# The second-last tile of a fused attention and MLP kernel, computed with tokens on the output partitions

## The chip, the cores and the metric

The kernel runs on one core of a Trainium2 chip. A core has five engines with an instruction stream each: TensorE (PE, matrix products), VectorE (DVE), ScalarE (ACT), GpSimd (POOL) and SyncE (SP, which here only starts transfers). ACT starts transfers too. Sixteen DMA engines move the data between the on-chip memory SBUF and the device memory. Matrix products are accumulated in PSUM, eight banks of 128 partitions by 512 float32.

The metric is the device time of one execution in microseconds. A profile of one execution shows what each engine did; its span runs from the first to the last recorded work, and the time of that execution is a little longer than the span.

## The reference

Polysketch attention over 4 batches, 4 heads, 1088 tokens and head size 32, and behind it a two-layer network with a leaky rectifier on the 4352 tokens of 128 features:

```python
def phi(x):
    a = np.einsum('rd,bhsd->bhsr', S1, x)
    b = np.einsum('rd,bhsd->bhsr', S2, x)
    return np.einsum('bhsi,bhsj->bhsij', a, b).reshape(*x.shape[:-1], r * r)
q_p, k_p = phi(q), phi(k)
kv = np.einsum('bhsf,bhsd->bhfd', k_p, v)
z = np.sum(k_p, axis=2)
num = np.einsum('bhsf,bhfd->bhsd', q_p, kv)
den = np.einsum('bhsf,bhf->bhs', q_p, z)[..., None] + 1e-06
x = (num / den).transpose(0, 2, 1, 3).reshape(B * S, H * D)
h = x @ w_in                                  # 128 -> 2048
g = np.maximum(h, 0.0) + alpha * np.minimum(h, 0.0)
out = g @ w_out                               # 2048 -> 128
```

## The kernel before

The kernel rewrites the rectifier as a linear part and a plain relu: `out = x @ W + relu(x @ w_in) @ ((1 - alpha) * w_out)` with `W = w_in @ (alpha * w_out)`. W is made on the chip (step Wmm and W).

**Steps of attention.** For each batch b the keys go through `k{b}T` (a transpose on DVE), `k{b}ab` (a product on PE, the two sketches), `k{b}abT`, two products `k{b}kp0` and `kp1` on POOL or DVE, the sums `z{b}` and `kv{b}` on PE, and `zm`, `zM`, `zW`, `kvc`, `fin`, `kvW`, which bring the sums into the form that the queries use. Queries go through `q{b}T`, `q{b}f` (PE), `fT`, `denm`, `den`, `rec`, `ph`, `phT` (DVE and POOL) and `q{b}num` (PE, line 838), and `q{b}x` copies the result to SBUF as the tile's input. Batch 0 is cut in parts (q0.a, q0.b, q0.1), since it starts while the inputs still arrive.

**Steps of the network.** `mlp` (from line 962) does one tile of tokens g, ten in all: tiles 0 to 5 and 7 have 512 tokens, 6, 8 and 9 have 256. d_ff is cut in 16 chunks. `h{g}.{c}` (line 982) is the first product of a chunk, with the weights stationary and up to 512 tokens streaming, into one PSUM bank; in tiles of 256 tokens two chunks share a bank. `r{g}.{c}` is the relu of that bank, on ACT (line 989) or DVE (line 991), to a bf16 buffer rh. `o{g}.{c}` (line 1004) is the second product, all chunks of which are added up in one bank, and `W{g}`, the linear part, is added to the same bank. The result of these tiles stands with the 128 output features on the partitions. `oT{g}` (line 1013, DVE) transposes it in blocks of 32 on its way to SBUF, and `st{g}` (`store_main`, line 1029) writes it with four transfers, one for each block of 32 features, so that one piece in device memory is 32 floats, 128 bytes. Tile 8's four transfers go two from SP and two from ACT.

Tile 9, the last, is done differently (`final`, line 1002): there the relu's output is stationary and the weights stream, 128 columns at a time, so that the result has tokens on the partitions. It takes twice as many matmuls of half the length, two PSUM banks, two plain copies (`oT9.0` on DVE, `oT9.1` on ACT, line 396 and 394) and two transfers with 512 bytes in one piece (`store_last`, line 1042), one from SP (`st9.0`) and one from ACT (`st9.1`).

**What sets the order.** A planner in the kernel (`plan`, line 188 on) orders all steps before any instruction is issued. Each step has a due time, worked back from its users, to which the table `SHIFT` adds a number for each step by name; a table `PIN` fixes the engine of some steps that two engines can do. The planner places steps by due time, by assumed durations, and by free buffers. Instructions then stand in that order on each engine, and each engine takes them strictly in order. SP's list holds all big loads and stores, ACT's the four small loads, the relus, copies and its stores. Loads of the weights from w_in1 on are released by the step zM0, those of batch 2 by kv1.0 and those of batch 3 by k2ab. The planner counts PE's instructions in blocks of 256 (`BLOCK`, `BEFORE`, line 58), because it reckons with the fetch of instructions; before the first tile it fills PE with warm-up matmuls (line 544).

The tile's own buffers: `po` is the bank for the second product (at most three at a time), `ph` a bank for a chunk (at most four), `oT__91` and `oT__92` in the profile are output buffers in SBUF, `ft__73` and `ph__75` are buffers of attention that tile 9 reuses.

Of the kernel before, what the change touches and what calls it, by code (L numbers as in the profile page):

```python
# [34 lines left out]
class Op:  # L35
# [274 lines left out]
def kernel(  # L310
# [12 lines left out]
    nc = tc.nc  # L323
# [41 lines left out]
    def ps(b):  # L365
        return PS[:, b.slot] if b.n == 1 else PS[:, b.slot:b.slot + b.n]

    def sb(b):
        return tiles[b.cls][b.slot]
# [592 lines left out]
    def mlp(g, n, xs, needs, bx, store, final=False, lat=5000):  # L962
# [32 lines left out]
        for i, (name, cs, z, dep, br, t) in enumerate(hs):  # L995
            def om(e, i=i, cs=cs, br=br, z=z):
                for q, c in enumerate(cs):
                    y, w = (xs(), W_bf) if c == NC else (sb(br)[:, q * np:q * np + np], w3[:, c, 0])
                    first, last = i + q == 0, i == len(hs) - 1 and c == cs[-1]
                    if final:  # L1000
                        for j in range(n // 128):
                            nc.tensor.matmul(ps(bos[j])[:, :128], y[:, 128 * j:128 * j + 128], w, start=first, stop=last)
# [118 lines left out]
```

## Time and profile before

| | |
|---|---|
| median of 3 runs | 105.85 us (105.42, 105.85, 107.14) |
| the profiled execution | 105.28 us |
| its span | 103.3 us |
| PE busy | 94.0 us, 91% |
| DVE, ACT, POOL busy | 83.9, 62.4, 43.1 us |
| granted clock of TensorE | 0.995 |
| moved by DMA | 11.83 MB, 26916 packets, of which 19988 under 512 bytes |

The page gives, in its parts, the busy time of each engine; the span in 40 slices of 2.6 us, with tenths of busy time for each engine; the DMA queues (q1 belongs to SP's transfers, q10 to ACT's, q8 and q14 carry instructions); the chain of work that ended last, by engine and line, where SPq and ACTq mean the issuing of a transfer; and the costliest groups of instructions. PE lists matmuls and PEld loads of stationary weights; both are TensorE instructions. In timelines a row is start in us, duration in us, engine, line, operation, output and input tiles, shapes and count; a bracket gives the idle time ahead and what ended it. The duration of several merged instructions is from the first start to the last end.

Matmuls of 512 columns follow each other every 0.217 us, and a pair of 256 takes the same. PE's last matmul starts at 98.69 us.

### The profile page before, as it was taken

The numbers are of one execution on the slowest core, as the hardware profiler recorded it, in microseconds if no ns is written. First come the engines' busy times: TensorE is split into PE (matmuls) and PEld (weight loads), VectorE is DVE, ScalarE is ACT, GpSimd is POOL, SyncE is SP. The second block draws the span as 40 slices with busy tenths as digits, with TensorE's granted clock in tenths as the row PEclk, the third lists the DMA queues.
The fourth block names the chain that finished last, engine by engine and source line by source line (L and its number), as shares of the span: only waits on it lengthen the run. The fifth ranks groups of instructions, "written<-read, shape, count | busy, mean of one in ns | idle before, by whom it ended". The sixth has DMA issues, their size and how long they took to land.

```text
span 103.3 us, 3390 instructions
## 1 busy us (share of the span) xinstructions
PE 94.0 (91%) x1374; PEld 54.7 (53%) x1384; DVE 83.9 (81%) x160; ACT 62.4 (60%) x134; POOL 43.1 (42%) x43
## 2 busy tenths in 40 slices
PE   7999898499799999999999999999999999999930
PEld 2348676276445745344364455554444765568920
DVE  6777789698978999799998959798896799849910
ACT  0604598997234896696296727746873757584610
POOL 3186885792896080195049239309900000000000
PEclk9999999999999999999999999999999999999997
DMA  2996689999002970199860001640000412410632
GB/s 33 341 260 161 221 259 342 367 196 167 14 6 74 381 191 8 19 341 271 122 111 0 0 0 27 114 74 0 0 0 9 75 24 41 83 30 5 109 51 53
DMA packets 26916, 11.83 MB, mean 115 GB/s; under 512 B 19988, under 2 KB 25364, under 8 KB 26900
## 3 DMA queue, kind: packets, MB, share of 16 engines
q1 hardware_dynamic: 25920, 11.44, 45.7%
q10 hardware_dynamic: 980, 0.16, 0.9%
q8 instruction: 11, 0.18, 0.7%
q14 instruction: 5, 0.04, 0.1%
HBM read 8.85 MB, written 2.23 MB: 107 GB/s over the span
## 4 chain that ended last, share of the span: by engine, by line
PE 76%; DMA 7%; DVE 6%; SPq 3%; issue 3%; ACTq 2%; ACT 0%; DVEq 0%
PE ps L982 27%; PE ps L1004 25%; DMA q<-in_q_dram 7%; PE ps L544 5%; PE ps L838 4%; PE ps L722 3%; PE ps L676 3%; PE ps L793 3%; SPq L417 3%; ACTq L1029 2%; PE ps L638 2%; DVE pt__77 L827 1%; DVE qT__71 L778 1%; PE ps L713 1%; PE ps L762 1%
## 5 line engine op out<-in xcount | busy, mean ns | idle before, releaser
L982 PEld LDWEIGHTS <-w_in_bf 128*128 128x128 bf16 x176 | 16.5, 98 | 14.1 <-issue 2.3
L1004 PEld LDWEIGHTS <-w 128*128 128x128 bf16 x160 | 15.4, 99 | 12.1 <-issue 1.6
L982 PE MATMUL ps<-xT__96,w_in_bf 128*128 128x512 bf16 (+1 forms) x78 | 19.8, 336 | 0.4 <-ACT xT__96 L394 0.2
L982 PE MATMUL ps<-xT__95,w_in_bf 128*128 128x512 bf16 (+1 forms) x79 | 18.8, 336 | 0.6 <-POOL w_in_bf L398 0.2
L989 ACT ACTIVATE rh__83<-ps 128x512 bf16<-128x512 f32 x17 | 10.3, 605 | 4.8 <-PE ps L982 3.4
L692 POOL TENSOR_TENSOR kp__68<-ab__66 128x1152 f32<-128x1152 f32 (+1 forms) x5 | 8.6, 1735 | 10.9 <-DVE ab__66 L679 8.9
L989 ACT ACTIVATE rh__84<-ps 128x512 bf16<-128x512 f32 x15 | 9.0, 598 | 3.8 <-PE ps L982 3.7
L989 ACT ACTIVATE rh__85<-ps 128x512 bf16<-128x512 f32 x15 | 9.0, 599 | 3.0 <-PE ps L1004 1.6
L1004 PE MATMUL ps<-rh__83,w 128*128 128x256 bf16 (+1 forms) x32 | 9.1, 326 | 0.2 <-issue 0.2
L824 POOL TENSOR_TENSOR ph__76<-ft__73 128x1280 f32<-128x1280 f32 x3 | 7.2, 2393 | 3.3 <-DVE ph__75 L824 3.3
L989 ACT ACTIVATE rh__86<-ps 128x512 bf16<-128x512 f32 x12 | 7.2, 601 | 1.6 <-PE ps L982 0.8
L1004 PE MATMUL ps<-rh__84,w 128*128 128x256 bf16 (+1 forms) x28 | 8.0, 325 | 0.2 <-issue 0.2
L544 PE MATMUL ps<-const-bfloat16-1.0 128*128 128x512 bf16 (+4 forms) x23 | 6.4, 380 | 0.9 <-PEq L1105 0.8
L991 DVE TENSOR_SCALAR rh__83<-ps 128x512 bf16<-128x512 f32 x9 | 6.1, 678 | 1.0 <-PE ps L982 0.8
L798 DVE STREAM_TRANSPOSE ft__73<-ps 128x576 f32<-128x576 f32 (+1 forms) x8 | 5.4, 703 | 1.8 <-PE ps L793 1.7
L989 ACT ACTIVATE rh__88<-ps 128x512 bf16<-128x512 f32 x11 | 6.6, 603 | 0.1
L692 POOL TENSOR_TENSOR kp__69<-ab__66 128x1152 f32<-128x1152 f32 x3 | 6.5, 2178 | 0.0
L838 PE MATMUL ps<-pt__77,kvW 32*32 32x256 f32 (+3 forms) x256 | 5.9, 372 | 0.6 <-DVE pt__77 L827 0.6
L1004 PE MATMUL ps<-rh__85,w 128*128 128x256 bf16 (+1 forms) x23 | 6.5, 323 | 0.0
L1004 PE MATMUL ps<-rh__86,w 128*128 128x512 bf16 (+1 forms) x21 | 6.5, 338 | 0.0
L991 DVE TENSOR_SCALAR rh__84<-ps 128x512 bf16<-128x512 f32 (+1 forms) x9 | 5.9, 653 | 0.4 <-PE ps L1004 0.2
L824 POOL TENSOR_TENSOR ph__75<-ft__73 128x1024 f32<-128x1024 f32 x2 | 3.9, 1950 | 5.4 <-DVE ft__73 L813 5.3
(175 smaller groups left out, 201.6 us busy)
## 6 DMA issues: line engine op xcount, KB each, us to landing
v<-in_v_dram SPq DMA_DIRECT2D x12, 144.0 KB, 5.8
k<-in_k_dram SPq DMA_DIRECT2D x3, 544.0 KB, 3.8
q<-in_q_dram SPq DMA_DIRECT2D x3, 544.0 KB, 7.6
out_dram<-oT__91 SPq DMA_DIRECT2D x20, 64.0 KB, 1.9
w_in_f<-in_moe_w_in_dram SPq DMA_DIRECT2D x4, 256.0 KB, 4.2
w_out_f<-in_moe_w_out_dram SPq DMA_DIRECT2D x2, 256.0 KB, 4.5
w_out_f<-in_moe_w_out_dram SPq DMA_DIRECT2D x1, 512.0 KB, 6.7
out_dram<-oT__92 SPq DMA_DIRECT2D x8, 64.0 KB, 3.3
```

The costliest lines, as they stand in the source:

```text
L417: (nc.sync if eng == "sp" else nc.scalar).dma_start(dst, src)
L544: nc.tensor.matmul(PS[:, 7, :n], ones(128), ones(n), start=True, stop=True, skip_group_check=True)
L676: nc.tensor.matmul(ps(pair)[32 * c:32 * c + 32, hp, :n], Wk[P].rearrange("p a b c -> p (a b c)"), x, start=True, stop=True, skip_group_che ...
L692: (nc.vector if e == "dve" else nc.gpsimd).tensor_tensor(out=dst, in0=i0, in1=i1, op=ALU.mult)
L722: nc.tensor.matmul(ps(bk)[32 * h:32 * h + 32, :R], v_sb[b][:, h, lo + s], at(sb(bkp[h // 2]), x, [[1, R]]), start=first and s == 0, stop=l ...
L798: nc.vector.transpose(at(sb(bf)[:, 0], 2 * y * D, [[D, 2], [H * D, ns], [1, D]]), ps(f2[y])[:, :, :n].rearrange("p h (s t) -> p h s t", t=D))
L824: (nc.vector if e == "dve" else nc.gpsimd).tensor_tensor(out=dst, in0=i0, in1=i1, op=ALU.mult)
L838: nc.tensor.matmul(ps(n2[c // 2])[32 * h:32 * h + 32, c % 2, :w * D], kvW[b][P, y, h], at(sb(bp)[P, 0], (2 * h + y) * D, [[2 * H * D, w], ...
L982: nc.tensor.matmul(ps(b)[:, k * np:k * np + np], w_in_bf[:, c * 128:(c + 1) * 128], xs()[:, z], start=k == 0, stop=c == cs[-1], skip_group ...
L989: nc.scalar.activation(sb(br)[:, :m], ps(b)[:, :m], ACTF.Relu)
L991: nc.vector.tensor_scalar_max(sb(br)[:, :m], ps(b)[:, :m], 0.0)
L1004: nc.tensor.matmul(ps(bo)[:, z], w, y, start=first, stop=last, skip_group_check=len(needs) > 1)
```

## The change

Tile 8 (256 tokens, the tile ahead of the last) is computed like tile 9, with tokens on the output partitions: for each chunk and for the linear part two matmuls of 128 columns, with the relu's output stationary, into two halves of one bank. One copy, on ACT or DVE as the planner chooses, takes the bank to SBUF in place of the transpose. Two transfers of 64 KB store it, with 512 bytes in one piece, one from SP and one from ACT; there were four of 32 KB with 128 bytes. The planner's cost for the steps o8 and W8 and its count of their instructions change with it.

```diff
                     if final:
                         for j in range(n // 128):
                             nc.tensor.matmul(ps(bos[j])[:, :128], y[:, 128 * j:128 * j + 128], w, start=first, stop=last)
+                    elif g == 8:
+                        for j in range(2):
+                            nc.tensor.matmul(ps(bo)[:, 128 * j:128 * j + 128], y[:, 128 * j:128 * j + 128], w,
+                                             start=first and j == 0, stop=last and j == 1, skip_group_check=True)
                     else:
                         nc.tensor.matmul(ps(bo)[:, z], w, y, start=first, stop=last, skip_group_check=len(needs) > 1)
...
-            o = op("pe", (62 * (k // 128) if final else k / 2.4 + 3) * len(cs), om, ...
-                   bos + [br], 200, t, name, ni=(k // 64 if final else 2) * len(cs))
+            o = op("pe", (62 * (k // 128) if final or g == 8 else k / 2.4 + 3) * len(cs), om, ...
+                   bos + [br], 200, t, name, ni=(k // 64 if final or g == 8 else 2) * len(cs))
...
+        if g == 8:
+            o = op(("act", "dve"), ad(256), lambda e: copy(e, sb(boT).rearrange("p a b -> p (a b)")[:, :256], ps(bo)[:, :256]), [last],
+                   [bo, boT], LA, end, "oT8")
+            for j in range(2):
+                op("act" if j else "sp", 640, lambda e, j=j: store(e, j, sb(boT)[:, j]), [o], [boT], 2100, end + 800, "st8act" if j else "st8sp")
+            return
         if not final:
             o = op("dve", dv(n) + 40, lambda e: nc.vector.transpose(bview(ob(boT), [[1, n]]), ps(bo)[:, :n]), [last],
                    [bo, boT], 80, end, f"oT{g}")
-            if g == 8:
-                for e, cut in (("act", (2, 3)), ("sp", (0, 1))):
-                    stores.append(op(e, 1150 if e == "act" else 950, lambda _, e=e, cut=cut: store(ob(boT), e, cut), [o], [boT], 2300, end + 800, f"st{g}{e}"))
-                return
...
+    def store_eighth(e, j, t):
+        (nc.scalar if e == "act" else nc.sync).dma_start(
+            bass.AP(tensor=out.tensor, offset=((B - 1) * S + 17 + 4 * j) * DM, ap=[[DM, 4], [NT * DM, 32], [1, DM]]), t)
...
-                mlp(g, 256, lambda bx=bx: sb(bx)[:, 1, :256], [res[c]], bx, store_main(b, c, 0, 256))
+                mlp(g, 256, lambda bx=bx: sb(bx)[:, 1, :256], [res[c]], bx, store_eighth)
```

The two tables are replaced whole: all 623 numbers of `SHIFT` are others (one name that no step used is gone), and `PIN` names 137 steps where it named 139, 113 entries being new, gone or different. So the planner gives another order. PE does the same steps with 32 more instructions (34 for tile 8, 2 warm-up instructions of its program fewer). On the other engines 48 relus and 15 other steps stand on another engine than before, among them S1sel (POOL, now DVE), w_in_bf0 and w_hi3 (POOL, now ACT), w_a0 (ACT, now POOL) and k0.1kp0 (DVE, now POOL). On SP the four transfers of tile 0's store stand ahead of the loads of batch 3; they stood behind them.

The order at the end, in the names of the steps (PE, then DVE, then ACT, then SP):

```
before, PE:  ... h9.2 o7.15 h9.4 W7 h9.6 o8.0 o8.2 o8.4 h9.8 o8.6 h9.10 o8.8 h9.12 o8.10 o8.12 h9.13 h9.14 h9.15 o8.14 W8 o9.0 ... W9 o9.14 o9.15
after,  PE:  ... h9.2 o7.15 h9.4 o8.0 h9.6 o8.2 h9.8 o8.4 h9.10 o8.6 h9.12 W7 o8.8 h9.13 o8.10 h9.14 o8.12 h9.15 o8.14 W8 o9.0 ... W9 o9.14 o9.15
before, DVE: ... r8.10 r8.14 oT7 r9.8 r9.12 r9.10 oT8 r9.14 r9.15 oT9.0
after,  DVE: ... r8.8 r8.10 r9.10 oT7 r9.14 r9.6 oT8 oT9.0
before, ACT: ... r9.0 r9.2 r9.6 r9.4 r9.13 st8act(2) oT9.1 st9.1
after,  ACT: ... r9.0 r8.12 r8.14 r9.2 r9.12 r9.4 r9.8 r9.13 r9.15 st8act(1) oT9.1 st9.1
both,   SP:  ... st6(8) st7(4) st8sp(2 before, 1 after) st9.0
```

More of the change, by code (lines that the diff above doesn't have):

```diff
@@ L66 @@
 SHIFT = {
[90 rows of a table removed]
[89 rows of a table added]
 }
 PIN = {
-    "S1sel": "pool", "Sq": "act", "k0.0kp0": "pool", "k0.0kp1": "pool", "k0.1kp0": "dve", "k0.1kp1": "pool",
-    "kvN": "act", "kvW2": "act", "kvW3": "dve", "kvc0": "act", "kvc1": "dve", "kvc2": "act", "kvc3": "act",
-    "kvn": "dve", "q0.1denm": "pool", "q0.1ph0": "dve", "q0.aRS": "act", "q0.bbc": "act", "q0.bfc": "dve",
[18 rows of a table removed]
+    "S1sel": "dve", "Sq": "act", "k0.0kp1": "pool", "k0.1kp0": "pool", "k0.1kp1": "pool", "kvW0": "dve",
+    "kvW1": "dve", "kvW2": "act", "kvW3": "dve", "kvc0": "dve", "kvc2": "dve", "kvn": "act", "q0.1denm": "pool",
[18 rows of a table added]
 }
@@ L1005, in mlp @@
             k = n if cs[0] == NC else np
-            o = op("pe", (62 * (k // 128) if final else k / 2.4 + 3) * len(cs), om, [dep, last] + ([] if cs[0] == NC else [c_wa[cs[0] // CP]]),
-                   bos + [br], 200, t, name, ni=(k // 64 if final else 2) * len(cs))
+            o = op("pe", (62 * (k // 128) if final or g == 8 else k / 2.4 + 3) * len(cs), om, [dep, last] + ([] if cs[0] == NC else [c_wa[cs[0] // CP]]),
+                   bos + [br], 200, t, name, ni=(k // 64 if final or g == 8 else 2) * len(cs))
             if cs[0] < NC:
@@ L1026, in store_main, with st @@
     def store_main(b, g, lo=0, n=512):
-        def st(t, e="sp", cut=range(4)):
-            for i in cut:
-                (nc.sync if e == "sp" else nc.scalar).dma_start(
-                    bass.AP(tensor=out.tensor, offset=(b * S + 17 * g) * DM + 32 * i, ap=[[NT * DM, 32], [DM, n // 32], [1, 32]]),
-                    bview(t[32 * i:32 * i + 32], [[32, n // 32], [1, 32]]))
+        def st(t):
+            for i in range(4):
+                nc.sync.dma_start(bass.AP(tensor=out.tensor, offset=(b * S + 17 * g) * DM + 32 * i,
+                                          ap=[[NT * DM, 32], [DM, n // 32], [1, 32]]),
+                                  bview(t[32 * i:32 * i + 32], [[32, n // 32], [1, 32]]))
         return st
```

215 rows, old and new, of tables (PIN, SHIFT) are left out of this document.

## The prediction

> **What bounds the kernel now.** I read the page's busy shares and slices first, then the chain that ended last, then the timeline of the last ten microseconds, then the single DMA issues.
>
> ```profile
> PE 94.0 (91%) x1374; PEld 54.7 (53%) x1384; DVE 83.9 (81%) x160; ACT 62.4 (60%) x134; POOL 43.1 (42%) x43
> ...
> PE   7999898499799999999999999999999999999930
> ...
> q8 instruction: 11, 0.18, 0.7%
> ...
> PE 76%; DMA 7%; DVE 6%; SPq 3%; issue 3%; ACTq 2%; ACT 0%; DVEq 0%
> ```
>
> TensorE (PE) is full from slice 9 on; only the first slices and the last two are not. So either PE's work or stalls must change, or the last 4 us. The end of the chain in order of time (start, us, what):
>
> ```profile
> 97.89 0.10 ACTq L1029
> 97.98 0.04 issue
> 98.03 1.74 ACTq L1029
> 99.77 0.04 issue
> 99.81 0.02 ACTq L394
> 99.82 0.04 issue
> 99.86 0.27 ACT ft__73 L394
> ```
>
> The last thing on the path is not PE: ScalarE (ACT) is issuing tile 8's second transfer for 1.74 us, and its copy of tile 9's second half waits behind that. The timeline of the tail:
>
> ```profile
> 94.44 0.71 DVE L1013 STREAM_TRANSPOSE oT__91<-ps 128x512 f32<-128x512 f32 x1
> ...
> 95.17 1.96 SPq L1029 DMA_DIRECT2D out_dram<-oT__91  x4
> ...
> 97.12 0.39 PE L1002 MATMUL ps<-w,rh__85 128*128 128x128 bf16 x4
> ...
> 97.35 0.39 PE L1002 MATMUL ps<-w,rh__84 128*128 128x128 bf16 x4
> ...
> 97.59 2.17 SPq L1029 DMA_DIRECT2D out_dram<-oT__92  x2
> ...
> 98.94 0.29 DVE L396 COPY ph__75<-ps 128x128 f32<-128x128 f32 x1 [0.74 <-PE ps L1002]
> 99.86 0.27 ACT L394 COPY ft__73<-ps 128x128 f32<-128x128 f32 x1 [2.60 <-DMA out_dram<-oT__92]
> 99.88 0.64 SPq L1042 DMA_DIRECT2D out_dram<-ph__75  x1
> 100.16 0.65 ACTq L1042 DMA_DIRECT2D out_dram<-ft__73  x1
> ```
>
> PE's last matmul ends at 98.96; the last two issues start at 99.88 and 100.16. The second lands 2.1 us later (DMA issue table: ft, 2.1), and the span closes 1.04 us after that: 3.14 us from start of issue to end.
>
> **Why two issues took 1.8 us.** The line's own view gives 388 and 1742 ns for ACT's two, 317 and 1812 ns for SP's two, of the same form. The trace's packet records show a transfer of 16,384 bytes on q8, the instruction queue, from 97.97 to 99.33; both issues begun around 97.97 end 0.43 us after it. Two other output stores are that slow, 2.39 us at 48.92 and 1.56 at 80.47, and beside each stands such a transfer (49.57 for 1.19, 80.34 for 1.27), ended 0.56 and 0.42 before the issue ended. Other issues of that form take 0.32 to 0.53. Eleven such transfers over PE's 2758 recorded instructions are one per 251: they follow PE's instruction count. I take it that a DMA issue met by one waits until about 0.45 us after its end.
>
> **Part by part**, in the profiled execution's time (span 103.30, and 1.98 outside it: 105.28).
>
> 1. *PE, tile 8's second product.* Seventeen steps of one 256-column matmul become two of 128. The first start every 0.109 (pairs of L1004, 94.17 and 94.39), the second every 0.056 (four of L1002 from 97.12 to 97.35): 17 x (0.113 - 0.109) = 0.06 us. 34 more PE instructions, less 2 of warm-up.
>    The Trainium skill, "TensorE: Matmul & The Clock Gate", section "Back-to-back issue gap", states about 81 ns for each 128-column matmul in a stream that alternates with weight loads. By it 34 of them would cost 0.85 us more than by the L1002 rows, and the sum would be 106.3; L1002 is just that stream in this trace and shows 56, so I keep the row.
> 2. *Evacuation of tile 8.* A copy instead of a transpose, both on VectorE (DVE): 0.42 (256-column copies at 14.50, 28.75) for 0.44. Nothing.
> 3. *Tile 8's store.* Four issues of 128-byte rows (317, 1812; 388, 1742 ns) become two of 512-byte rows, the form of L1042: 0.64 each. ACT is then free before PE ends, so its copy can start at 99.0 and its last store at 99.3 rather than 100.16: 0.86 us gained on ACT's side. What is late next is SP.
> 4. *SP, tile 7's store.* The new order moves W7, the last matmul of tile 7, from behind h9.4 to behind h9.12: seven more matmul steps of 0.217 and h9.12 of 0.11, 1.63 us, so W7 at 93.74 + 1.63 = 95.37 and its end at 95.75. DVE also puts r9.10 ahead of the transpose oT7 (h9.10 ends at 95.23, the relu then holds DVE 0.6: 95.9). oT7 ends at 96.6 where it ended at 95.15. SP issues in order: st7's four, tile 8's, tile 9's. Without a stall that is 96.6 + 1.96 + 0.68 = 99.25, just when tile 9's copy is ready (98.96 + 0.29): hidden, with nothing to spare.
> 5. *The instruction transfer.* 32 PE instructions more by then bring it forward by 16 matmul-and-load pairs of 0.056: from 97.97 to about 97.1, until 98.4 (1.36). Now SP is in the middle of st7: first issue 96.6 to 96.95, the second held until 98.87, third and fourth (0.51 each) until 99.99, tile 8's until 100.67, tile 9's from 100.7. ACT's store is held only until 98.9, and ACT's copy follows at 99.0. So SP now ends last, 0.82 later than before (99.88) and 0.54 later than ACT's old last issue. Bounds: 99.28 (nothing held) to 101.2 (the transfer catches the first issue too). I take 100.7, since all three output issues that met one were held.
> 6. *From the last issue to the end.* Above, 3.14, by a store that stood behind tile 8's small rows. Here packets start 0.85 after issue (st7: 95.17 to 96.0 in the packet records), drain 0.5 and land 0.26 later, then 1.04: 2.65. Lower end: the 16 KB stores' 1.5 to landing, 2.54. I take 2.65: 103.35.
> 7. *The rest of the plan.* All planned times are replaced, 48 relus change between ACT and DVE, and 15 other steps change engine. PE's order keeps its skeleton: q1num, k2ab, q2num, k3ab, q3num, h6.0, h7.0, h8.0 and o9.0 have the same PE work ahead of them as before, so the sum of PE's work is the same and only waits can differ. Of those I followed the ones on long chains. S1sel goes from GpSimd (POOL, 0.40 at 5.85) to DVE ahead of zm0: zM0, which releases the loads from w_in1 on, some 0.1 to 0.3 later; DMA is full (share 1.00 from 14 to 21 us), so the q load on which PE waits 1.38 us at 18.5 shifts as much. I take 0.1. w_hi3 moves to ACT ahead of r0b.12 and r0b.14 (1.26 us); its cover is the wait of PE for the transpose pt__77 until 27.5, and uncovered it costs up to 0.1. The third and fourth of the phT transposes for q2 and q3 end before their matmuls (59.65 for 60.0; 77.9 for 78.2). Store 0 goes to SP ahead of k3, which is released at 42.5, when store 0 (four issues from about 38.5) is out: nothing; uncovered it would eat from the 2 us that k3 waits for its transpose at 48.28.
>
> Sum: 103.35 + 0.1 = 103.5 span (0.06 of PE lies under SP's queue), **105.5 us**. The median shown, 105.85, is 0.57 above the profiled execution; the three runs spread over 1.7, so I leave the forecast on the profiled one. Two per cent, 2.1 us, is about what a measurement of this kernel can tell from no change.
>
> **Rivals.**
> *The gain is not eaten.* If the transfer does not hold SP, or falls before 95, the last SP store starts at 99.28; with 3.14 the span is 102.4 and the time 104.4, with 2.54 it is 103.8, and less where PE's 1.8 us of idle time between 21 and 99 (busy time by stretches) shrinks: 103.3. For it: issues at 95.53 and 96.06 passed a smaller transfer (8 KB on q14, 95.79) without harm. Against: three of three. The Trainium skill, "Runtime: NRT & Kernel Launch", section "Instruction fetch mechanics", states that instructions come in 16 KiB blocks of 256 by the sequencer's own DMA queue and that the crossing is mostly hidden; by that rule this rival holds, and in this trace the size agrees while the issues beside it say it is not hidden from DMA.
> *PE loses in the hand-over of PSUM banks (slower).* Six places in the new order (h1.7, h4.4, h6.10, h6.14, h7.14, h9.14) reuse a bank with only 0.76 to 0.97 us of PE work since its last matmul; drain 0.16, relu 0.60 and two hand-overs need about 0.86. If at each place ACT is one relu (spacing 0.49) behind, 2.9 us: 108.4; at half of them 106.9. It decides above 2% only when five of six miss. Against: ACT is 60% busy and 0.49 apart at worst.
> *The change does what it says but PE's end moves with the loads:* the q load 0.6 later (an issue at 9.32 took 1.03 beside the transfer at 9.05, so such a slip is possible): 106.0, inside the range.
>
> **How the numbers follow.** Forecast 0.57 (own range 104.9 to 106.1, with late loads); gain not eaten 0.25 (103.3 to 104.8); PE loses 0.18 (106.1 to 108.4). Range 103.7 to 107.6: it leaves out the low third of the second and two thirds of the last, 0.2 in all. Faster by over 2% (under 103.73): 0.09, that low third. Slower by over 2% (over 107.97): 0.11, the upper part of the last. Within: 0.80.
>
> **What would show it.** ACT's 2.60 wait gone and its last store starting near 99.3; oT7 ending near 96.6; one long issue inside st7; the L1050 store on SP starting near 100.7 as the chain's last; tile 8's matmuls 0.056 apart; PE ending within 0.3 of 98.96. Wrong if no store issue after 96 exceeds 0.7 us, if PE ends past 99.8, or if the last issue to end takes over 3.2.

## The result and the profile after

| | before | after |
|---|---|---|
| median, 20 executions each | 105.75 us | 106.82 us |
| lowest to highest | 104.66 to 107.99 | 105.64 to 108.82 |
| the profiled execution | 105.28, span 103.3 | 105.64, span 103.6 |

The ratio of the times, over executions that were not disturbed, is 1.0105 with a 95% interval of 1.0074 to 1.0136: the change makes the kernel about 1.1 us slower. That is less than 2%, but the interval is clear of 1, and it goes against the forecast, which stood a little below the median. The profiled execution of the changed kernel is its fastest of all; two more profiles of the same code, taken later, have a span of 104.9 each. The first profile alone would mislead, so the section on the experiments reads all three.

Lines of the changed kernel's page that answer to those shown of before (part 1, two of the slices, the instruction queue, and the chain by engine):

```profile
PE 95.2 (92%) x1400; PEld 55.0 (53%) x1400; DVE 78.3 (76%) x154; ACT 66.6 (64%) x141; POOL 43.8 (42%) x42
...
PE   7997999599899999999999999999999999999920
...
q8 instruction: 11, 0.18, 0.7%
...
PE 77%; DMA 7%; ACT 4%; DVE 4%; SPq 3%; issue 2%; ACTq 0%; DVEq 0%
```

The share of ACTq on the chain has gone from 2% to nothing. The end of the same kernel's chain shows why: it now runs from PE straight into ACT's copy, without a store issue in between.

```profile
97.26 1.92 PE ps L1000 x34
99.19 0.02 issue
99.21 0.02 ACTq L392
99.22 0.04 issue
99.26 0.27 ACT ft__73 L392
```

The tail in the same kernel's timeline (start, duration, engine, line, operation; L1021, L1033, L1046 and L1050 are the lines of the transpose, the main store, tile 8's new store and tile 9's store):

```profile
96.10 0.70 DVE L1021 STREAM_TRANSPOSE oT__91<-ps 128x512 f32<-128x512 f32 x1
96.83 2.90 SPq L1033 DMA_DIRECT2D out_dram<-oT__91  x4
98.08 0.62 ACTq L1046 DMA_DIRECT2D out_dram<-oT__92  x1
98.90 0.28 PE L1000 MATMUL ps<-w,rh__85 128*128 128x128 bf16 x2
99.22 0.29 DVE L394 COPY ph__75<-ps 128x128 f32<-128x128 f32 x1 [1.18 <-PE ps L1000]
99.26 0.27 ACT L392 COPY ft__73<-ps 128x128 f32<-128x128 f32 x1 [0.87 <-PE ps L1000]
99.56 0.61 ACTq L1050 DMA_DIRECT2D out_dram<-ft__73  x1
99.83 0.70 SPq L1046 DMA_DIRECT2D out_dram<-oT__92  x1
100.65 0.63 SPq L1050 DMA_DIRECT2D out_dram<-ph__75  x1
```

ACT's copy no longer waits 2.60 us for a transfer but 0.87 for PE. Tile 7's store, four issues, takes 2.90 where it took 1.96: its third issue alone takes 1.48, beside an instruction transfer on q8 from 97.87 to 98.80. Everything behind it on SP is late, and the last store starts at 100.65 although its data were there at 99.51.

### The profile page after: what moved, and what is told of

It reads as the page before. It is cut to its first block, busy times and chain, and to the rows that moved or that the text cites. A ratio compares the mean times of both kernels' runs of the same rounds, so it can differ in the third digit from the quotient of the medians.

```text
span 103.6 us, 3424 instructions
## 1 busy us (share of the span) xinstructions
PE 95.2 (92%) x1400; PEld 55.0 (53%) x1400; DVE 78.3 (76%) x154; ACT 66.6 (64%) x141; POOL 43.8 (42%) x42
## 4 chain that ended last, share of the span: by engine, by line
PE 77%; DMA 7%; ACT 4%; DVE 4%; SPq 3%; issue 2%; ACTq 0%; DVEq 0%
PE ps L980 26%; PE ps L1006 24%; DMA q<-in_q_dram 7%; PE ps L542 5%; PE ps L836 4%; PE ps L720 3%; PE ps L791 3%; SPq L415 3%; PE ps L674 2%; PE ps L1000 2%; PE ps L1003 2%; PE ps L636 2%; DVE pt__77 L825 1%; DVE qT__71 L776 1%; ACT w L613 1%
## 5 line engine op out<-in xcount | busy, mean ns | idle before, releaser
L980 PEld LDWEIGHTS <-w_in_bf 128*128 128x128 bf16 x176 | 16.6, 98 | 12.7 <-issue 1.4
L1006 PEld LDWEIGHTS <-w 128*128 128x128 bf16 x144 | 14.1, 99 | 12.7 <-issue 2.0
L980 PE MATMUL ps<-xT__96,w_in_bf 128*128 128x512 bf16 (+1 forms) x80 | 20.6, 337 | 0.1
L980 PE MATMUL ps<-xT__95,w_in_bf 128*128 128x512 bf16 (+1 forms) x80 | 20.3, 337 | 0.1
L987 ACT ACTIVATE rh__83<-ps 128x512 bf16<-128x512 f32 (+1 forms) x18 | 10.7, 595 | 4.5 <-PE ps L980 4.4
L987 ACT ACTIVATE rh__85<-ps 128x512 bf16<-128x512 f32 (+1 forms) x17 | 10.2, 600 | 3.0 <-PE ps L980 2.9
L987 ACT ACTIVATE rh__87<-ps 128x512 bf16<-128x512 f32 x15 | 9.1, 609 | 3.5 <-PE ps L1006 2.5
L987 ACT ACTIVATE rh__84<-ps 128x512 bf16<-128x512 f32 x16 | 9.7, 609 | 1.1 <-PE ps L1006 0.8
L1006 PE MATMUL ps<-rh__83,w 128*128 128x512 bf16 (+1 forms) x31 | 9.1, 331 | 0.0
L1006 PE MATMUL ps<-rh__84,w 128*128 128x512 bf16 (+1 forms) x30 | 8.7, 329 | 0.1
L822 POOL TENSOR_TENSOR ph__76<-ft__73 128x1280 f32<-128x1280 f32 (+1 forms) x3 | 6.7, 2243 | 3.3 <-DVE ph__75 L822 3.3
L989 DVE TENSOR_SCALAR rh__84<-ps 128x512 bf16<-128x512 f32 x9 | 6.2, 683 | 2.3 <-PE ps L980 2.3
L987 ACT ACTIVATE rh__88<-ps 128x512 bf16<-128x512 f32 (+1 forms) x12 | 7.0, 585 | 1.2 <-PE ps L980 0.7
L1006 PE MATMUL ps<-rh__85,w 128*128 128x512 bf16 (+1 forms) x24 | 7.2, 335 | 0.2 <-ACT rh__83 L987 0.2
L989 DVE TENSOR_SCALAR rh__83<-ps 128x512 bf16<-128x512 f32 x8 | 5.4, 680 | 2.3 <-ACT rh__87 L987 2.3
L987 ACT ACTIVATE rh__86<-ps 128x512 bf16<-128x512 f32 x10 | 6.0, 600 | 1.5 <-PE ps L980 1.5
L836 PE MATMUL ps<-pt__77,kvW 32*32 32x256 f32 (+3 forms) x256 | 5.9, 372 | 0.2 <-DVE pt__77 L825 0.2
L1006 PE MATMUL ps<-rh__86,w 128*128 128x512 bf16 (+1 forms) x18 | 5.7, 344 | 0.0
```

The costliest lines, as they stand in the source:

```text
L822: (nc.vector if e == "dve" else nc.gpsimd).tensor_tensor(out=dst, in0=i0, in1=i1, op=ALU.mult)
L836: nc.tensor.matmul(ps(n2[c // 2])[32 * h:32 * h + 32, c % 2, :w * D], kvW[b][P, y, h], at(sb(bp)[P, 0], (2 * h + y) * D, [[2 * H * D, w], ...
L980: nc.tensor.matmul(ps(b)[:, k * np:k * np + np], w_in_bf[:, c * 128:(c + 1) * 128], xs()[:, z], start=k == 0, stop=c == cs[-1], skip_group ...
L987: nc.scalar.activation(sb(br)[:, :m], ps(b)[:, :m], ACTF.Relu)
L989: nc.vector.tensor_scalar_max(sb(br)[:, :m], ps(b)[:, :m], 0.0)
L1006: nc.tensor.matmul(ps(bo)[:, z], w, y, start=first, stop=last, skip_group_check=len(needs) > 1)
```

## The experiments

To place a step or a warm-up freely, the planned order of each kernel was written out as a list in place of the planner; unless said otherwise all steps keep engine, place and buffers. "Ratio" is always to the kernel before, run on the same chip in the same session, with a 95% interval.

To compare profiles whose loads arrive at different moments, each span is cut in three: S, up to the start of the first product of the queries with kvW (L838, L836 in the changed code); P, from there to the end of PE's last matmul; and T, from there to the end of the span. All three are read from the timeline and the span. In four profiles of the kernel before, P is 71.42 to 71.43, so a difference in P of a tenth means something. S varies in both kernels with the loads (26.9 to 28.6 in fourteen of the seventeen profiles, 29.4 to 31.9 in the others). The granted clock is 1.00 in all seventeen from before the start of P to PE's end, so P and T can be set side by side also where S is long. The span is given to a tenth, so T is good to about 0.05.

**1. The store of tile 7 early again.** The changed kernel with three steps moved back to where they stood:

```diff
-PE:  h9.4 o8.0 ... h9.12 W7 o8.8 ...
+PE:  h9.4 W7 o8.0 ... h9.12 o8.8 ...
-DVE: r9.10 oT7        SP: st7 behind oT7
+DVE: oT7 ... r9.10    SP: st7 behind oT7
```

> The changed kernel with three steps of the end moved back: W7 directly behind h9.4 on PE, oT7 directly behind it (so ahead of r9.10 on DVE), and st7 issued with it; nothing else moves. Theory A (the time is lost in SP's list at the end, tile 7's store being late and meeting the instruction transfer): st7 issues from about 95.1 to 97.0, clear of the transfer at 97.9; the two stores of tile 8 start near 98.1 and are not held; the last two stores start at 99.3 to 99.6; span 1.0 to 1.2 shorter than the changed kernel's, ratio to the kernel before 0.995 to 1.0. Theory B (the time is lost earlier, by the new order before 90 us): the tail is shorter in the profile by the same steps, but the median stays at 1.005 or above; if PE's last matmul also moves, B is right in that part. Theory C (PE waits in PSUM banks): no change, 1.01.

Measured: ratio 0.9999 [0.9945, 1.0053]. T is 3.64 where the changed kernel has 4.43. So the late store of tile 7 is worth about 1 us of the changed kernel's time, as theory A has it (0.8 by T against the first profile, 1.1 against the mean of three; 1.3 by the ratio beside that of the fourth run). Its profile had a late start (S 31.88), which doesn't touch P and T.

**2. The edit alone.** The new code for tile 8, with every step on the engine and in the place of the kernel before.

> The edit alone: the new code for tile 8 (matmuls of 128 columns, copy, two stores of 512-byte rows), with every step on the engine and in the place that it had before, so the two tables change nothing. Theory A: PE ends near 99.1 as before plus 0.1, ACT's 2.60 wait goes, the last issues start at 99.3 to 99.9, span 102.3 to 102.7, ratio 0.990 to 0.995. Theory B: the same or a little better, as all of the loss is the tables'. Theory C with the 32 more PE instructions as the cause (later waits at banks, or more instruction fetch): ratio 1.0 or above.

Measured: 1.0016 [0.9957, 1.0075]; T 3.74, P 71.47, S 29.39. The tail is shorter by 0.6 than in the first profile of the kernel before, just as theory A says, and the time isn't. This run was repeated twice, below, where its late start is looked at as well.

**3. The tables alone.** The code of before, the order of the changed kernel.

> The two tables alone: every step on the engine and in the place that the changed kernel gives it, but tile 8 computed as before, with a transpose and four stores of 128-byte rows. Theory A: SP has st7 late as in the changed kernel, then two held small-row issues, then tile 9's store: span 103.9 to 104.8, ratio 1.010 to 1.018 (no better than the changed kernel). Theory B: the loss before 90 us is here in full, ratio 1.005 to 1.015, and PE's last matmul stands as late as in the changed kernel. Theory C with the edit as the cause: ratio below 1.005.

Measured: 1.014 [1.0048, 1.0231]; T 4.94, but P is also up, at 72.07. Theory A has the size right, and theory B is right in part: PE itself has lost 0.64 before the tail.

**4. The changed kernel again**, for a second profile.

> The changed kernel once more, as the measure for the three others on the same chip and for a second profile. All theories: ratio 1.007 to 1.014. Theory A: its profile shows PE's last matmul no later than in the kernel before, and the last store on SP more than 1 us behind it. Theory B: where this profile is longer than the first (103.6), PE's last matmul is late by the difference.

Measured: 1.0125 [1.0026, 1.0224]; P 72.27, T 4.89. Set beside the first profile, matmul by matmul, the two run in step from 20 us on but for one place. In the first profile (timeline of PE):

```profile
51.09 0.38 PE L760 MATMUL ps<-ident,bs__100 128*128 128x128 f32 x2
51.62 0.38 PE L980 MATMUL ps<-xT__96,w_in_bf 128*128 128x512 bf16 x1
```

and in the second:

```profile
51.31 0.38 PE L760 MATMUL ps<-ident,bs__100 128*128 128x128 f32 x2
52.46 0.38 PE L980 MATMUL ps<-xT__96,w_in_bf 128*128 128x512 bf16 x1 [0.77 <-issue]
```

The bracket says that PE waited 0.77 us for nothing that the profile shows. Where nothing disturbs, these two steps are 0.22 apart (fifth run, below), so even the first profile has 0.31 of it.

The trace's packet records point to a cause. A 16 KB transfer on q8 ends at 50.32 in the first profile and 50.93 in the second; PE goes on 1.30 and 1.53 later. In the run of the tables alone it ends at 50.64 and PE goes on 1.58 later. Counted back from this place, 256 of PE's records (matmuls and weight loads) reach to the burst of small matmuls at 46.2 (L711). Theory F: PE has used up a block of 256 instructions in about 5 us (the new order puts the 64 instructions of q1f and the 128 of kv1.0 side by side in it), and the next block isn't there yet, because its transfer starts some 3 us after that border, at 49.1 to 49.9. In the kernel before the transfer comes as late after the border there (3.4 to 3.7 us, counted in the same way), but PE takes 7.3 to 7.4 us for the block.

**5. The border moved later.** The changed kernel with 22 fewer warm-up instructions (the numbers are the units of 32 columns of warm-up ahead of a step):

```diff
-fill: rowsT 2, k0.1ab 14, z0.0 4, z0.1 20, zM0 4, q0.aw 4, kv0.1 11, q0.aR 1, fin0 4
+fill: rowsT 0, k0.1ab 16, z0.0 0, z0.1 16, zM0 0, q0.aw 0, kv0.1 8,  q0.aR 0, fin0 0
```

> The changed kernel with 22 fewer warm-up instructions of PE before 20 us (11 short warm-up matmuls with their weight loads); every step keeps its place. This moves each border of PE's 16 KB instruction blocks 11 matmuls later. Theory F (in the new order one block is used up in 5.2 us, from 46.4 to 51.6, because q1f, 64 instructions, stands just ahead of kv1.0, 128 instructions; its successor is asked for at 49.1 to 49.9 only, and PE waits for it from 51.7 to 52.2 or 52.5, as in the second profile of the changed kernel): the border falls at about 54.0 instead of 51.6, the wait of 0.77 marked issue at L980 is gone, and the median is 0.4 to 0.8 below the changed kernel's, ratio to the kernel before 1.004 to 1.009. Rival (that wait has another cause, a bank or a relu): the wait stays, ratio 1.010 to 1.014. In the tail the transfer moves 0.6 later and still meets the store of tile 7, so nothing is gained there by either theory.

Measured: 0.9967 [0.9916, 1.0018]. The wait is gone (timeline of PE):

```profile
52.07 0.38 PE L760 MATMUL ps<-ident,bs__100 128*128 128x128 f32 x2
52.29 0.38 PE L980 MATMUL ps<-xT__96,w_in_bf 128*128 128x512 bf16 x1
```

P falls from 72.27 to 71.32, which is 0.11 less than in the kernel before. So the rest of the new order costs PE nothing here. T is 4.27; tile 7's store is held as before, now at its fourth issue (1.13 us). The ratio fell below the expected 1.004 to 1.009; part of that is the tail, which came out at 4.27 instead of the 4.75 that the changed kernel's three profiles have in the mean.

**6. Both.** The same, with W7, oT7 and st7 early.

> The same 22 warm-up instructions taken out, and W7, oT7 and st7 early as in the first experiment. Theories A and F together: the two gains add, 1.3 from the tail and 0.4 to 0.8 from the block: span of undisturbed runs 102.4 to 102.9, ratio 0.992 to 0.996, which is faster than both kernels. If only the tail matters: 1.000, as the first experiment.

Measured: 0.9942 [0.989, 0.9994], median 105.63 beside 106.34 of the kernel before in that session. P 71.39, T 3.66. The two gains add; this version is faster than both kernels, if by little. Its tail (timeline):

```profile
95.06 1.96 SPq L1033 DMA_DIRECT2D out_dram<-oT__91  x4
98.09 0.70 SPq L1046 DMA_DIRECT2D out_dram<-oT__92  x1
98.10 0.61 ACTq L1046 DMA_DIRECT2D out_dram<-oT__92  x1
99.63 0.61 ACTq L1050 DMA_DIRECT2D out_dram<-ft__73  x1
99.65 0.63 SPq L1050 DMA_DIRECT2D out_dram<-ph__75  x1
```

The instruction transfer stood at 97.85 to 99.14. Both stores of tile 8 were issued in the midst of it and neither was held.

**7. The kernel before with its last border moved.** Code and order of before, 22 warm-up instructions fewer.

> The kernel before with 22 fewer warm-up instructions; every step keeps its place. The border of the last instruction block moves 11 short matmuls later, and with it the transfer from 97.97 to 98.6 or later. Theory A (a store issue of 128-byte rows that meets this transfer is held until about 0.45 after its end): tile 8's second issues, 1812 and 1742 ns before, take about 0.5, ACT's copy starts at 99.0 instead of 99.86, and the time is 0.6 to 0.8 lower, ratio 0.992 to 0.995, without any of the change's edits. Rival (these issues are slow for another reason, such as two queues writing at once): they stay near 1.8 and the ratio is 1.000.

Measured: 0.9933 [0.9876, 0.9989]. The last transfer fell behind the end of the span; the page lists ten where the others have eleven. Queue row and tail:

```profile
q8 instruction: 10, 0.16, 0.7%
```

```profile
96.95 0.81 SPq L1029 DMA_DIRECT2D out_dram<-oT__92  x2
96.95 0.89 ACTq L1029 DMA_DIRECT2D out_dram<-oT__92  x2
98.41 0.27 ACT L394 COPY ft__73<-ps 128x128 f32<-128x128 f32 x1 [1.79 <-PE ps L1002]
98.66 0.63 SPq L1042 DMA_DIRECT2D out_dram<-ph__75  x1
98.71 0.65 ACTq L1042 DMA_DIRECT2D out_dram<-ft__73  x1
```

The same four issues that took 317, 1812, 388 and 1742 ns in the kernel before take 0.81 and 0.89 us in pairs, T is 3.68 instead of 4.34, and P is 71.42 as ever. In the tail that is the whole gain of the edit, without the edit. It shows that the transfer held these issues: nothing else in the tail was touched. This one execution is no measure of the time, though: it took 104.93, which is 2.9 us more than its span, where every other execution with a span on record, the eleven others of this kernel included, took 2.0 to 2.2 more. Its late transfer stands at 103.99 to 105.17, behind the span; whether that is why was not tried.

**8 and 9. The edit alone, twice more.**

> The edit alone on the old order, once more, since its first profile was one with a late start. Theory A as before: the end of the span 3.7 after PE's last matmul instead of 4.3, ratio 0.994. If the edit itself costs PE something, PE's last matmul stands later by 0.5 or more than in the kernel before at an equal start, and the ratio is 1.00.

> The edit alone on the old order, a third time, for a closer ratio (1.0016 and 0.9969 so far). If the 0.6 of the tail that both profiles show reaches the time: 0.994, pooled about 0.997. If the edit costs PE or the loads something of the same size: 1.000.

Measured: 0.9969 [0.9923, 1.0014] and 0.9988 [0.9936, 1.0039]; with the first, 0.9991 in the mean. T is 3.78 and 3.77, as expected, but P is 72.08 and 72.28. Both have a wait inside the 32 matmuls of q0's second part, at the border of an earlier block. From the third run's timeline:

```profile
28.55 0.97 PE L791 MATMUL ps<-qT__71,Wq 32*32 32x288 f32 x8
29.77 0.75 PE L791 MATMUL ps<-qT__71,Wq 32*32 32x288 f32 x24 [0.26 <-issue]
```

The bracket counts only 0.26, since the matmul ahead is drawn as long; by the starts, the burst lasts 1.39 and 1.58 us instead of 0.66, so the waits are 0.7 and 0.9. The transfer ended at 28.28 and 28.30, and PE went on at 29.77 both times: 1.49 and 1.47 later, the same lag as at 52.

The first run of the edit has such a wait too, ahead of P. From its timeline:

```profile
12.89 0.27 PE L720 MATMUL ps<-kp__70,v 128*32 128x64 f32 x2 [1.01 <-issue]
```

A transfer ended at 11.60 there, 1.30 before PE went on. So each of the three profiles of the edit has a wait of 0.7 to 1.0 at some block border, more than the 0.4 by which its T is under the mean of the kernel before. Behind that place PE of the first run still waits 1.2 us for a transpose (kT, at L674), so how much of the block wait reaches the end is not known.

**10. The border moved earlier.** The changed kernel with 20 more warm-up instructions (matmuls of 512 columns cut in two):

```diff
-    return [512] * (units // 16) + [256] * (units % 16 // 8) + ...
+    return [256] * (units // 8) + ...
```

> The changed kernel with 20 more PE instructions before 20 us (ten warm-up matmuls of 512 columns cut into two of 256, so PE's work there is the same); every step keeps its place. The opposite of the run with 22 fewer. Theory F: the block border that stood at 51.6 now falls at the end of kv1.0, near 50.1, while the transfer of the next block still starts at 49.1 to 49.9 and is of use only 1.3 to 1.6 after its end: PE waits 1.6 to 2.4 just behind kv1.0 where it waited 0.1 to 0.85, and the ratio to the kernel before rises to 1.018 to 1.025. Rival (fewer warm-ups helped in another way, or the wait has another cause): ratio as the changed kernel's, 1.010 to 1.014, and no wait near 50.

Measured: 1.0068 [1.0013, 1.0123]. The wait moved as theory F says, from behind L760 to the end of kv1.0:

```profile
51.36 0.30 PE L720 MATMUL ps<-kp__69,v 128*32 128x64 f32 x3 [0.90 <-issue]
```

Its size was missed: P is 72.52, 1.2 above the run without the wait, not 1.6 to 2.4. The transfer started at 48.74 here, 0.4 to 1.1 earlier than in the other profiles of this order, and ended 1.39 before PE went on. The ratio was missed as well; the span's parts would give 1.012, at the interval's upper end. So the place of the wait is shown to follow the border; that its size follows the moment of the transfer, which this kernel doesn't control, is an inference from the lag. PE's records show the border by themselves: counted from the first, the matmul that waits is number 1716 in the changed kernel's three profiles, in those of the first and third runs, and again in this run, although another step stands there. In the edit's runs it is number 952 (twice) and 442, which is three and five blocks of 256 ahead but for four and six records.

**11. The changed kernel a third time.**

> The changed kernel a third time, for another profile. Theory F with A: the wait marked issue at L980 near 52 is there with 0.4 to 0.9, one or two of tile 7's store issues are held until about 0.45 after the transfer, span end 4.4 to 4.9 after PE's last matmul, ratio 1.008 to 1.014.

Measured: 1.010 [1.0038, 1.0163]; P 71.97, T 4.92. By the starts, PE lost 0.58 at L980 and 0.16 in the burst near 30 us, and made up some of it. Tile 7's second issue took 1.95 us here and 1.77 in the second profile, the third 1.48 in the first.

**12 to 14. The kernel before, three more profiles.**

> The kernel before once more, for a second profile. If the wait at the block border near 29.1 is a matter of the single execution: it is seen in one or two of the three looks, with the transfer ahead of it starting later than 27.0. If it came with the edit: no wait there in any of the three, and the transfer starts at 26.0 to 26.7.

> The same again: a third profile of the kernel before, judged with the second. In all three the last issues of tile 8 on SP and ACT take 1.2 to 1.9 each, and the span ends 4.2 to 4.5 after PE's last matmul.

> The same again: a fourth profile of the kernel before, judged with the second and third.

Measured: no wait at 29 us in any; the burst lasts 0.66 in all four profiles of the kernel before, P is 71.42 to 71.43. The transfer ahead of it ended at 27.33 to 27.59 in three of them, 0.7 to 1.0 before it did in the two runs of the edit that waited. T is 4.34, 3.69, 4.36 and 4.21. The 3.69, outside the expected 4.2 to 4.5, is from an execution whose clock was granted in full only from 16.8 us on (S 31.38): there the transfer took only 0.88, and the held issues (1.16 and 1.09) were over 0.15 us after PE's end.

**15. The edit alone with 22 fewer warm-ups.**

> The edit alone on the old order, with 22 fewer warm-up instructions. The block border moves 11 matmuls later, behind the burst at 29.1, where the next block has been there for some time. If the wait there ate the gain of the edit: no wait of PE marked issue from 28 to 55, span end 3.7 after PE's last matmul, ratio 0.991 to 0.995. If something else ate it: 0.998 to 1.001 as without.

Measured: P 71.48, T 3.77, no wait marked issue. The times scattered (104.12 to 107.27, median 105.91 beside 105.88), and no usable ratio came of it. The wait is gone with the border moved, but whether the gain reaches the time stays open.

**All together.** P + T against the mean of the kernel before (75.58), over 105.75, beside the measured ratio:

| kernel | P | T | P + T would give | measured |
|---|---|---|---|---|
| before, four profiles | 71.43 | 3.69 to 4.36 | 1 | 1 |
| changed, three profiles | 71.63, 72.27, 71.97 | 4.43, 4.89, 4.92 | 1.011 | 1.0105, 1.0125, 1.010 |
| tables alone | 72.07 | 4.94 | 1.014 | 1.014 |
| changed, tile 7's store early | 72.08 | 3.64 | 1.001 | 1.000 |
| changed, border later | 71.32 | 4.27 | 1.000 | 0.997 |
| changed, both | 71.39 | 3.66 | 0.995 | 0.994 |
| changed, border earlier | 72.52 | 4.35 | 1.012 | 1.007 |
| edit alone, three profiles | 71.47, 72.08, 72.28 | 3.74, 3.78, 3.77 | 1.001 | 0.999 |
| before, last border away | 71.42 | 3.68 | 0.995 | 0.993 |

With the profiles of a version averaged, two terms, the wait for an instruction block on PE and the length of the tail, account for every ratio within its interval (the border moved earlier only just). The changed kernel loses some 0.5 us by the first and 0.6 by the second (4.75 in the mean against 4.15). The intervals are 0.3 to 1.0 us wide to each side, about as large as each term, so the table tests the sum better than the parts, and a single profile can stand outside that of its own run: the first of the changed kernel alone would give 1.005, the second and third of the edit 1.003 and 1.004. Without the profile with the 3.69 the mean of the kernel before is 75.73, and every figure of the column falls by 0.001. The edit with 22 fewer warm-ups would stand at 0.997, with no ratio to set beside it.

## Why the prediction was wrong

*Step 1, PE's cost of tile 8.* Right: 0.06 expected; P is 71.47 in the edit's first run, which had no wait within P, 0.04 above before. Matmuls of 128 columns start every 0.056 at L1003 as at L1000. The Trainium skill, "TensorE: Matmul & The Clock Gate", section "Back-to-back issue gap", gives 81 ns in such a stream; by that, P would have been 0.85 higher, and it wasn't.

*Steps 2 and 3.* Right. The copy costs what the transpose did (0.41 for 0.44); ACT's last store starts at 99.56 instead of 100.16, and the new store on ACT was not held.

*Step 4, tile 7 late.* Right: oT7 was to end at 96.6 and ended at 96.80. That this order, not the edit, takes the tail's gain away is shown by the first run.

*Step 5, the transfer inside st7.* Right in kind: an issue of tile 7's store is held in all three profiles. That the last store was found at 100.65, where 100.7 was expected, is luck: in that profile the transfer started at 97.87 instead of 97.1, lasted 0.93 instead of 1.36 and held the third issue instead of the second. From PE's end (98.96) to that start the step had 1.74; the three profiles have 1.48, 1.89 and 2.00.

*Step 6, issue to end.* Too small: 2.65 expected; 2.95, 2.96 and 2.94 measured. The parts were taken from tile 7's store of the kernel before; why tile 9's takes longer, with tile 8's just ahead of it on the queue, was not tried. With both last stores issued together it is 3.2 to 3.4 (102.9 - 99.65 in the sixth run).

*Step 7, the rest of the plan, +0.1.* **This is the step that failed.** "The sum of PE's work is the same and only waits can differ" was true, and P without waits is even 0.04 to 0.11 lower; but the list of waits that was then followed held data only. That the 16 KB transfers follow PE's instruction count was in the prediction, ahead of its step 5, and was used for the stores alone: a wait of PE itself for its next block, when the order packs 192 small instructions into one, was put at nothing. The waits came to 0.3 to 0.95 in every one of the five profiles of this order with the border in its place (P less 71.32: 0.31, 0.95, 0.65, 0.75, 0.76; part of the 0.65 is the 0.16 near 30 us). In the mean of the changed kernel's three profiles P is 0.53 over the kernel before, where the step had 0.1. The source that the step named for its 0.1 isn't seen either: with S1sel on DVE the first load of w_in is issued at 8.58 to 8.84 in the changed kernel's three profiles, and at 8.95 to 9.20 in three of the kernel before, so it is earlier, not later.

*The base.* The forecast was left on the profiled execution, 105.28; the median of 20 is 0.47 above it. With the 0.43 that step 7 lacked and the 0.36 by which T was too short (4.39 expected, 4.75 in the mean; 0.30 of it is step 6), that makes up the 1.3 by which 105.5 fell short of 106.82. The base also turned the sign: on its own profile the sum says 0.2 slower, but beside the median shown, 105.85, the same 105.5 reads as faster. And 2% was not the least that could be told: the interval of the ratio is 0.3% to each side.

*What would show it.* In the first profile nearly all of it came true, so that profile alone would have spoken for the account. The second and third have the sign of being wrong that the prediction named: PE ends at 100.01 and 99.98, past 99.8.

*The rivals.* "PE loses in the hand-over of PSUM banks" gave the right sign for the wrong reason: none of the six places shows a wait, and P without block waits is lower than before. "The gain is not eaten" is what the first and sixth runs and the edit's tails show, T 3.64 to 3.78; its price by the last issue's 3.14, a span of 102.4, is a T of 3.44, 0.2 to 0.35 too short. Late loads: S is 27.41 to 27.86 in three profiles of before and 27.54 to 28.01 in the changed kernel's; nothing can be read from that.

The Trainium skill, "Runtime: NRT & Kernel Launch", section "Instruction fetch mechanics", says that crossing a 16 KiB boundary is mostly hidden. In the kernel before it was, for PE (P 71.43 in all). In the changed kernel it wasn't: 0.31 to 0.95 us at one border, and moving the border by 22 instructions made it go away.

What stays open: why the edit's three profiles have a block wait (at 12.9 in one, near 29 in two, where the transfer started at 27.2 and not, as in three profiles of the kernel before, at 26.45, 25.39 and 26.28) and the four of the kernel before none. The order up to there is the same, instruction for instruction, which speaks for chance, but three of three against none of four doesn't settle it.

## What to carry to other kernels

A new order of many small PE instructions is to be costed twice: for the data and for PE's own instruction blocks. Count 256 instructions from border to border, read off how long the order takes for them, and compare with when the q8 transfer of the next block ends in the trace, plus about 1.4 us; where the trace says "issue" ahead of a matmul, this is the first thing to look at. Before rewriting a tile to get a store out of the way of such a transfer, try moving the transfer: taking out 22 warm-up instructions did here for the tail what the whole edit did (T 3.68 against 3.74 to 3.78).

## What the runs showed of the hardware

In ten profiles issues of 128-byte rows met the last 16 KB instruction transfer. In each of them one issue, or one on each queue, lasted until 0.35 to 0.45 us after the transfer's end, 1.02 to 1.95 us in all, where such an issue takes 0.31 to 0.54 otherwise in the tail of the kernel before. Not each was held: four that began from 0.13 before to 0.30 after the transfer's start took 0.32 to 0.51. Issues of 512-byte rows begun in the midst of such a transfer took 0.61 to 0.70 in all of twelve cases, the same as without. That the row size, and so the number of pieces, makes the difference is an inference; no run changed it alone.

A fetched instruction block was of use to PE 1.30 to 1.58 us after its packets had ended, in nine waits. Counted in records, in the thirteen profiles with no warm-ups taken out, the fetch began 0.5 to 1.5 us after the border in 52 of 65 cases between 28 and 70 us, and 0.35 to 2.3 after it in all; at the border at 46 us it began 2.2 to 3.9 after it. The count is not exact: near 81 us the fetch begins about 1 us ahead of the counted border in twelve of the thirteen. Loads of batches 2 and 3 are under way near 46 us; that they are the reason was not tried.
